# Splitting the first loads of a one-core kernel over three DMA queues

## The chip, the cores and the metric

One core of one Trainium2 chip runs the kernel. Times are device microseconds (us). Five engines work beside each other, each with its own list of instructions: TensorE (PE; its weight loads are the row PEld), VectorE (DVE), ScalarE (ACT), GpSimd (POOL) and SyncE (SP). DMA transfers are issued by SP, ACT or GpSimd, each into a queue of its own, and are carried out by 16 DMA engines. Rows with a "q" behind the engine (SPq, ACTq) are issues or waits of an engine's sequencer.

## What is computed

The input x has 2048 rows of 512. A gate per row mixes two branches:

```python
x = A_x
g = _sigmoid((x * gate_w).sum(-1, keepdims=True))
a = _A_ref(x, A_Lambda_re, A_Lambda_im, A_B_re, A_B_im, A_C_re, A_C_im, A_log_dt, A_Dskip)
b = _B_ref(x, B_wqkv, B_w_phi, B_wo)
return g * a + (1 - g) * b
```

Branch A is a diagonal complex state space model with 512 states: `Bu = x B_bar^T`, a recurrence `h = Lam_bar * h + Bu[t]` over the 2048 rows, and `y = 2 Re(h C^T) + x * Dskip`. Branch B is linear attention with 32 heads of 16: q, k and v come from `x @ wqkv`; q and k go through `w_phi` and a pair of softmaxes (of p and of -p); `kv` and `z` are sums over all rows; the output is `num / den` times `wo`. All inputs are bf16.

## The kernel before

**Tiling.** The rows are dealt by their place modulo 8, and 16 tiles of 128 rows (x0 to x15) are loaded by DMA transposes into `xT` (partition = input column). The helper `x_load(ti)` at L228 issues one such transpose on SP's queue. B's weight halves (real and imaginary, 512 KB each) go to `Bn` and from there, by eight more DMA transposes, to `BT`.

**An order written by hand.** The steps are generators (`st_...`), and the string `ORDER` (L24) lists them in the order in which their parts are emitted. The order of instructions on TensorE, VectorE, ScalarE and SP is the order of emission; GpSimd's instructions are placed by the scheduler. A token such as `W1@0` runs the next part of step W1 with PSUM bank 0; `:D` puts an eviction on VectorE instead of ScalarE; `F:4` emits four filler products (128x128 on a tile of ones, L812) that nobody reads. Every DMA issue is in order on its engine too.

**The opening.** Before the string is read, L164 issues K's weight in two halves (256 KB each, into a tile named C2r) on ACT's queue, L166 issues `w_phi` (16 KB, into Wc) on SP's, L167 preloads a ScalarE table, L236 to L240 issue x0 to x3, V's weight `Wv` (512 KB) and x4 to x7 on SP's queue, and L251 issues five small loads (vec_n, vec_m) on GpSimd's. In the string:

- `NR`, `NI` (st_N, L283) issue the two halves of B on SP's queue; `l8` to `l15` issue the other x tiles; `R0` to `R7` (st_BT, L287) the transposes of B.
- `B` (L342) builds BD, a block-diagonal matrix of w_phi, on VectorE. `W0` to `W3` (L271) transpose K's weight on TensorE; `f0` to `f3` (fold, L428) multiply it by BD, which gives Wk2.
- `V` (L308) transposes vec_n on TensorE and copies it to `vec`: the decay's parameters. `P`, `P2` to `P4`, `U` and `i0` to `i3` work on it on VectorE and ScalarE.
- `k0` to `k15` and `v0` to `v15` (tile_mm, L473) are four products of 128x512 each on one x tile; `x0`, `n0`, `e0`, `s0` and so on are the softmax features of groups of tiles (two, two, four, four, four), on VectorE and ScalarE; `a0` (L571) is the first product on features (kvacc). `g00` and so on (L597) are branch A's products on BT.
- `M` (L379) is a chain of small operations on GpSimd: powers of the decay. Three of them (r2_, r4_, r8_, L397 to L399) depend on step P alone. `D` (L417) is the reader of M's result on VectorE (dg).

Of the kernel before, what the change touches and what calls it, by code (L numbers as in the profile page):

```python
# [10 lines left out]
ALU = mybir.AluOpType  # L11
# [9 lines left out]
P = 128  # L21
MAGIC = 12582912.0
Z_MAX = 70.0
ORDER = """  # L24
NR F:28 NI B W1@0 W0@1 W0 W2@2 W1:D W3@3 W3 f1@4 W2:D f0@5 f2@6 f0 f1:D l10 V@0 F:4 V P f3@1 f3 f2:D F:4 P P k1@2 k1
l13 P2 k0@3 P2 U P2 P2 P2 P2 P4 k2@4 P3 P3 k3@5 P4 P4 k0 v0@0 i0 i2 U i0 i0 i1 i2 k4@7 i0:D i0 k2 i2 i2:D i2 U k3 k5@6
i1 v3@1 n0 x0 l9 i1 V2@2 i3 l12 x0 k4 v2@3 i3 i3 l14 i1 k5 n0 x0 n0 x0 i3 k7@4 n0 x0 U n0 i1 l11 k6@5 n1 x1 x1 n1 x1
n1 l8 R0 R1 x1 i3 k7 M v7@7 x1 n1 n1 k6:D L V2 v1@6 x2 n2 e0 v6@4 v5@5 v4@2 e0 x2 s0 v0 l15 n2 s0 n2 v2 s0 v1 R2 s0 v6
v3 n2 k10@0 k10 s0 k9@3 k9 C4 k13@6 gw D R3 s0 k12@4 e1 v7 s0 e1 s1 C6 k11@1 k11 x2 s1 k14@0 k8@3 k12 k14 k8 v4 k13
# [39 lines left out]
def kernel(  # L69
# [18 lines left out]
    nc = tc.nc  # L88
    _, S, D = A_x.shape
# [6 lines left out]
    NR = 8  # L96
# [29 lines left out]
    def order_after(ins, earlier, why):  # L126
        tc.add_manual_dep(ins.ins, earlier.ins.name, NOSYNC, reason=why)

    def pin_act_set():
        pre = nc.scalar.preload_act_table_set(ACT_SET)  # L130
        for s_ in act_st["sins"]:
            order_after(pre, s_, "table set after trig")
        act_st["pre"] = pre
        act_st["sins"] = []
        act_st["exps"] = []

    def aexp(**kw):
        ins = nc.scalar.activation(**kw)  # L138
        order_after(ins, act_st["pre"], "Exp/Ln after table-set preload")
        act_st["exps"].append(ins)  # L140
        return ins
# [19 lines left out]
    Wv = const.tile([P, KT, D], BF16, name="Wv")  # L161
    wk_nat = const.tile([P, KT, D], BF16, name="C2r")
    C2r = wk_nat
    for k0 in (0, 2):  # L164
        nc.scalar.dma_start(out=wk_nat[:, k0:k0 + 2, :], in_=B_wqkv[k0 * P:(k0 + 2) * P, D:2 * D].rearrange("(k p) n -> p k n", p=P))
    nc.sync.dma_start(out=Wc[:], in_=B_w_phi.rearrange("(k hl) e f -> (hl e) k f", hl=8))  # L166
    pin_act_set()  # L167

    xT = const.tile([P, KT, S], BF16, name="xT")
    Wo = const.tile([P, KT, D], BF16, name="Wo")  # L170
# [8 lines left out]
    G = const.tile([P, NTI], F32, name="G")  # L179
# [28 lines left out]
    Bn = pBC.tile([P, NT2, D], BF16, name="Bn")  # L208
# [19 lines left out]
    def x_load(ti):  # L228
        nc.sync.dma_start_transpose(out=xT[:, :, ti * P:(ti + 1) * P], in_=x_res[ti // 2, ti % 2])  # L229
# [3 lines left out]
    make_identity(nc, identf[:])  # L233
    mask16 = stg.tile([P, 8], BF16, name="mask16", bufs=1)
    nc.vector.tensor_reduce(out=mask16[:], in_=identf[:].rearrange("p (g e) -> p g e", e=16), axis=AX.X, op=ALU.max)
    for ti in range(4):  # L236
        x_load(ti)
    nc.sync.dma_start(out=Wv[:], in_=B_wqkv[:, 2 * D:3 * D].rearrange("(k p) n -> p k n", p=P))
    for ti in range(4, 8):
        x_load(ti)  # L240
    fk_g = tc.tile_pool(name="featK", bufs=3, reuse_waits="tile")
    fk = fk_g.__enter__()
# [21 lines left out]
    dt_, r_, om_, t0, t1, t2, den_, r2_, r4_, om8, r8_ = (par[:, 10 + k, :] for k in range(11))  # L264
    GT = nc.gpsimd.tensor_tensor
    m16 = maskN[:].rearrange("p a b -> p (a b)")
    order = [2 * g + q for g in ORD for q in range(2)]
    live = {}
# [12 lines left out]
        yield  # L281

    def st_N(ri):  # L283
        nc.sync.dma_start(out=Bn[ri * 64:(ri + 1) * 64, :, :], in_=(A_B_re, A_B_im)[ri].rearrange("(t p) d -> p t d", p=64))  # L284
        yield

    def st_BT(t):  # L287
# [16 lines left out]
    def st_O():  # L304
        nc.sync.dma_start(out=Wo[:], in_=B_wo.rearrange("(k p) n -> p k n", p=P))
        yield

    def st_V():  # L308
        pvt = bank([P, 12], BF16, "pvt")
        nc.tensor.transpose(pvt[:], vec_n[:], ident[0:12, 0:12])  # L310
        yield
        nc.vector.tensor_copy(out=vec[:, 0:3, :].rearrange("p n j -> p (n j)"), in_=pvt[:])
        yield
# [61 lines left out]
    def st_gw():  # L375
        nc.vector.tensor_copy(out=gw_b[:], in_=vec[:, 4, :])
        yield

    def st_M():  # L379
        GS = nc.gpsimd.tensor_scalar  # L380
        GC = nc.gpsimd.tensor_copy

        def cross(a, b):
            GT(out=outer, in0=a.unsqueeze(2).to_broadcast([P, 2, 2, PT]), in1=b.unsqueeze(1).to_broadcast([P, 2, 2, PT]), op=ALU.mult)

        def cmul(k, a, b):
            cross(a, b)
            GT(out=dl[:, k, :], in0=outer[:, 0, 0], in1=outer[:, 1, 1], op=ALU.subtract)
            GT(out=dl[:, k + 1, :], in0=outer[:, 0, 1], in1=outer[:, 1, 0], op=ALU.add)

        lb, m2, m4 = dl[:, 0:2, :], dl[:, 2:4, :], dl[:, 4:6, :]
        GT(out=dl[:, 0, :], in0=cs_, in1=r_, op=ALU.mult)
        GT(out=dl[:, 1, :], in0=sn_, in1=r_, op=ALU.mult)
        cmul(2, lb, lb)
        cmul(4, m2, m2)
        cmul(6, m2, m4)
        GT(out=r2_, in0=r_, in1=r_, op=ALU.mult)  # L397
        GT(out=r4_, in0=r2_, in1=r2_, op=ALU.mult)
        GT(out=r8_, in0=r4_, in1=r4_, op=ALU.mult)  # L399
        cross(lb, lam)  # L400
        GT(out=tb[:, 0, :], in0=outer[:, 0, 0], in1=outer[:, 1, 1], op=ALU.subtract)
        GT(out=tb[:, 1, :], in0=outer[:, 0, 1], in1=outer[:, 1, 0], op=ALU.add)
        GT(out=tb, in0=tb, in1=lam, op=ALU.subtract)
        GT(out=dl[:, 9, :], in0=tb[:, 0, :], in1=den_, op=ALU.mult)
        GT(out=dl[:, 8, :], in0=tb[:, 1, :], in1=den_, op=ALU.mult)
        lo = dl[:, 0:10, :].rearrange("p (k t) j -> p k t j", t=2)
        up = dl[:, 10:20, :].rearrange("p (k t) j -> p k t j", t=2)
        GS(out=up[:, 0:4, 0], in0=lo[:, 0:4, 1], scalar1=-1.0, scalar2=None, op0=ALU.mult)
        GC(out=up[:, 0:4, 1], in_=lo[:, 0:4, 0])
        GS(out=up[:, 4, 0], in0=lo[:, 4, 0], scalar1=-1.0, scalar2=None, op0=ALU.mult)  # L410
        GC(out=up[:, 4, 1], in_=lo[:, 4, 1])
        for h in range(2):
            for ri in range(2):
                GC(out=dgB[ri * 64:(ri + 1) * 64, :, :, h], in_=dl[h * 64:(h + 1) * 64, 10 * ri:10 * ri + 10, :])
        yield

    def st_D():  # L417
        v5_ = dgv.rearrange("p (k t a) f -> p k t a f", k=4, a=2)
        b5_ = dgB[:, 0:8].rearrange("p (k a) j h -> p k a (j h)", a=2)
        for a in range(2):  # L420
            nc.vector.tensor_copy(out=v5_[:, :, :, a, :], in_=b5_[:, :, a, :].unsqueeze(3).to_broadcast([P, 4, NT2, 4]))
        VT(out=idn2[:], in0=ident[:, 0:64], in1=ident[:, 64:P], op=ALU.add)
        VT(out=dg[:].rearrange("p k t (a c f) -> p (k t a) c f", f=4, a=2),
           in0=idn2[:].rearrange("p (c f) -> p c f", f=4).unsqueeze(1).to_broadcast([P, 8 * NT2, 16, 4]),
           in1=dgv.unsqueeze(2).to_broadcast([P, 8 * NT2, 16, 4]), op=ALU.mult)
        yield
# [250 lines left out]
    def st_G():  # L677
        VS(out=nge[:], in0=live["acc"][1][:, 4 * KVW:4 * KVW + NTI], scalar1=-Z_MAX, scalar2=-1.0, op0=ALU.max, op1=ALU.mult)
        yield
        aexp(out=G[:], in_=nge[:], func=ACT.Exp)  # L680
        yield
        VS(out=G[:], in0=G[:], scalar1=1.0, scalar2=None, op0=ALU.add)
        yield
        nc.vector.reciprocal(out=G[:], in_=G[:])
        yield

    def st_Y():
        for b in range(2):
# [72 lines left out]
    def st_t(n):  # L761
# [8 lines left out]
        else:  # L770
# [5 lines left out]
    small1, big1 = (lambda: sk), (lambda: fk)  # L776
    small3, big3 = (lambda: pools["sq"][1]), (lambda: pools["eq"][1])
    st = {"V": st_V(), "V2": st_V2(), "U": st_U(), "P": st_P(), "P2": st_P2(), "P3": st_P3(), "P4": st_P4(), "B": st_B(), "gw": st_gw(),
          "M": st_M(), "D": st_D(), "L": st_L(), "G": st_G(), "Y": st_Y(), "END": st_END(), "NR": st_N(0), "NI": st_N(1), "O": st_O()}
    for n in range(8, NTI):  # L780
        st[f"l{n}"] = st_l(n)
    for j in range(4):
# [65 lines left out]
```

## Time and profile before

| | |
|---|---|
| Time, median of 3 runs | 155.59 us (154.87 to 156.52) |
| Span of the profiled execution | 153.2 us |
| Busy: PE, PEld | 146.2 us (95%), 95.0 us (62%) |
| Busy: DVE, ACT, POOL | 132.4 us (86%), 129.2 us (84%), 15.8 us (10%) |
| Mean granted TensorE clock | 0.995 |
| Moved by DMA | 17.55 MB, mean 115 GB/s |

The profile is of one execution. A timeline row gives the start, the duration (of a merged group, from its first start to its last end), engine, line, operation, tiles (out<-in, buffer numbers left out), shapes, count, and in brackets the engine's idle time before it and what ended it. A busy TensorE isn't TensorE at its peak: products overlap, and a 128x512 product shown with 379 ns can follow the one before it after 216 ns.

### The profile page before, as it was taken

The page shows a single profiled execution, that of the slowest core. Times are in us where ns is not written, and L with a number is a line of the kernel's source. Part 1 is how long each engine was busy: PE and PEld are TensorE (multiplying, and loading weights), DVE is VectorE, ACT ScalarE, POOL GpSimd, SP SyncE. Part 2 cuts the span into 40 slices and gives each one's busy share as a digit, 9 for nine tenths or more (in the row PEclk, how much of TensorE's full clock was granted, in tenths as well). Part 3 has the DMA queues.
Part 4 walks back from the last instruction along what each step waited for, and adds up shares of the span by engine and source line. Part 5 has one row for each costly group of instructions (what it writes and reads, how often), then busy time and mean ns, then how long its engine had stood idle before and what let it go on. Part 6 is the DMA issues. An engine that isn't in the chain of part 4 may idle for free.

```text
span 153.2 us, 3361 instructions
## 1 busy us (share of the span) xinstructions
PE 146.2 (95%) x1236; PEld 95.0 (62%) x1254; DVE 132.4 (86%) x303; ACT 129.2 (84%) x279; POOL 15.8 (10%) x43
## 2 busy tenths in 40 slices
PE   7899999999999999999999999999999999999990
PEld 7644434788878985869867656555554455555540
DVE  3799999999999999999999999999999958717520
ACT  3489998999998999999998999699498998627562
POOL 8239980000000000000000000000000000000000
PEclk9999999999999999999999999999999999999997
DMA  4875995534445699930000007711278859969842
GB/s 116 164 218 97 223 178 112 103 75 103 103 107 78 129 230 178 166 115 4 0 0 4 0 0 169 74 37 34 42 98 147 176 122 189 162 129 206 247 143 103
DMA packets 50848, 17.55 MB, mean 115 GB/s; under 512 B 44176, under 2 KB 50832, under 8 KB 50832
## 3 DMA queue, kind: packets, MB, share of 16 engines
q1 hardware_dynamic: 48976, 15.75, 53.8%
q10 hardware_dynamic: 1696, 1.57, 3.2%
q8 instruction: 10, 0.16, 0.5%
q0 software_dynamic: 160, 0.01, 0.2%
q14 instruction: 6, 0.05, 0.1%
HBM read 2.64 MB, written 2.10 MB: 31 GB/s over the span
## 4 chain that ended last, share of the span: by engine, by line
PE 78%; SPq 10%; DMA 7%; issue 1%; ACT 1%
PE pgq L601 18%; PE py L717 16%; PE pq L475 9%; PE py L765 8%; SPq L229 8%; PE pv L475 4%; PE ph L668 4%; PE pk L475 4%; DMA xT<-in_A_x_dram 4%; PE kvacc L578 3%; DMA phT<-EEq 3%; PE pn L736 3%; PE pgq L606 2%; PE py L722 2%; PE pgq L608 2%; SPq L284 1%
## 5 line engine op out<-in xcount | busy, mean ns | idle before, releaser
L601 PE MATMUL pgq<-xT,BT 128*128 128x256 bf16 x256 | 31.5, 272 | 0.0
L475 PEld LDWEIGHTS <-xT 128*128 128x128 bf16 x192 | 18.2, 98 | 18.3 <-DMA xT<-in_A_x_dram 0.7
L601 PEld LDWEIGHTS <-BT 128*128 128x128 bf16 x256 | 24.6, 98 | 4.1
L138 ACT ACTIVATE EEk<-EEk 128x1024 bf16<-128x1024 bf16 x20 | 20.4, 1080 | 0.0
L119 ACT CAST uv<-pgq 128x512 bf16<-128x512 f32 x28 | 15.9, 605 | 0.5 <-PE pgq L601 0.4
L475 PE MATMUL pv<-Wv,xT 128*128 128x512 bf16 x59 | 15.5, 379 | 0.3
L475 PE MATMUL pq<-Wq,xT 128*128 128x512 bf16 x60 | 15.4, 379 | 0.2
L765 PE MATMUL py<-Wo,oT 128*128 128x512 bf16 x62 | 15.3, 379 | 0.1
L475 PE MATMUL pk<-Wk,xT 128*128 128x512 bf16 x62 | 14.7, 379 | 0.3 <-DMA xT<-in_A_x_dram 0.2
L138 ACT ACTIVATE EEq<-EEq 128x1024 bf16<-128x1024 bf16 x12 | 11.7, 1042 | 0.3 <-DVE EEq L527 0.3
L769 ACT ACTIVATE ot<-py,G 128x512 bf16<-128x512 f32 x12 | 7.9, 686 | 4.5 <-PE py L765 4.3
L138 ACT ACTIVATE ld<-pn 128x16 f32<-128x16 f32 x32 | 6.1, 191 | 5.7 <-PE pn L736 4.6
L590 ACT ACTIVATE phT<-X,dgB 128x512 bf16<-128x512 bf16 x16 | 10.7, 725 | 0.0
L119 ACT CAST nu<-pn 128x256 bf16<-128x256 f32 x27 | 9.9, 380 | 0.0
L119 ACT CAST vx<-pv 128x512 bf16<-128x512 f32 x16 | 9.1, 604 | 0.4 <-PE pv L475 0.4
L548 DVE TENSOR_TENSOR EEk<-EEk,rck 128x4096 bf16<-128x4096 bf16 (+1 forms) x5 | 9.3, 1858 | 0.0
L744 DVE TENSOR_TENSOR on<-nu,rd 128x512 bf16<-128x512 bf16 x16 | 6.7, 421 | 2.8 <-ACT rd L138 1.6
L765 PEld LDWEIGHTS <-oT 128*128 128x128 bf16 x64 | 5.7, 97 | 5.3 <-DMA oT<-on 0.5
L119 ACT CAST Xq<-pq 128x512 bf16<-128x512 f32 x16 | 8.9, 608 | 0.0
L119 ACT CAST Xq<-pk 128x512 bf16<-128x512 f32 x15 | 8.6, 598 | 0.4 <-PE pk L475 0.4
L736 PEld LDWEIGHTS <-phT 128*128 128x128 bf16 x128 | 6.2, 97 | 3.8 <-DMA phT<-EEq 1.4
L511 DVE TENSOR_TENSOR smk<-smk 128x512 bf16<-128x512 bf16 (+4 forms) x18 | 8.1, 448 | 0.1
(178 smaller groups left out, 321.2 us busy)
## 6 DMA issues: line engine op xcount, KB each, us to landing
X<-HM SPq DMA_DIRECT2D x8, 256.0 KB, 4.5
out_dram<-ot ACTq DMA_DIRECT2D x8, 128.0 KB, 2.5
out_dram<-ot SPq DMA_DIRECT2D x8, 128.0 KB, 2.2
C2r<-in_B_wqkv_dram ACTq DMA_DIRECT2D x2, 256.0 KB, 3.8
Wv<-in_B_wqkv_dram SPq DMA_DIRECT2D x1, 512.0 KB, 4.0
Bn<-in_A_B_re_dram SPq DMA_DIRECT2D x1, 512.0 KB, 5.7
Bn<-in_A_B_im_dram SPq DMA_DIRECT2D x1, 512.0 KB, 6.8
Wo<-in_B_wo_dram SPq DMA_DIRECT2D x1, 512.0 KB, 4.3
```

The costliest lines, as they stand in the source:

```text
L119: nc.scalar.copy(out=out_ap, in_=in_ap)
L138: ins = nc.scalar.activation(**kw)
L229: nc.sync.dma_start_transpose(out=xT[:, :, ti * P:(ti + 1) * P], in_=x_res[ti // 2, ti % 2])
L475: MM(out=pt[:], lhsT=xT[:, kt, ti * P:(ti + 1) * P], rhs=W[:, kt, :], start=(kt == 0), stop=(kt == KT - 1))
L511: VT(out=dst, in0=cur[:, :, :, 0:n, :], in1=cur[:, :, :, n:2 * n, :], op=op)
L548: VT(out=E5, in0=E5, in1=rc.to_broadcast([P, L, 2 * NB, Dh, 4]), op=ALU.mult)
L590: nc.scalar.mul(out=t_, in_=x_, mul=c_)
L601: MM(out=pg[:, h, :], lhsT=BT[:, kt, 2 * j + h, :], rhs=xT[:, kt, r * NC:(r + 1) * NC], start=(h == 0 and kt == 0), stop=(r % 2 == 0 and k ...
L717: MM(out=py[:], lhsT=hs(r, t, slice(a * P, (a + 1) * P)), rhs=C2B[t], start=(t == 0), stop=False)
L736: MM(out=pn[:, 4 * m:4 * m + 4, :].rearrange("p h e -> p (h e)"), lhsT=ph[:, 4 * hf + m, :], rhs=KVm[:, 4 * hf + m, :], start=(m == 0), st ...
L765: MM(out=py[:], lhsT=oT[:, g, :], rhs=Wo[:, g, :], start=False, stop=(g == HG - 1))
L769: nc.scalar.mul(out=ot[:], in_=py[:], mul=G[:, ti:ti + 1])
```

## The change

K's weight is issued in two halves on two queues at once: the first on ACT's, the second as the first issue of SP's, ahead of w_phi. V's weight moves from the middle of SP's x tiles to ACT's queue, right behind the table preload. The halves of B move from SP's queue to GpSimd's, behind the three powers of the decay, which become a step of their own, MP. SP's queue then carries x0 to x7 without a break. In the string, NR and NI stand behind MP, k0 comes before k1, and of the eight filler products around V and P two are left.

```diff
 ORDER = """
-NR F:28 NI B W1@0 W0@1 W0 W2@2 W1:D W3@3 W3 f1@4 W2:D f0@5 f2@6 f0 f1:D l10 V@0 F:4 V P f3@1 f3 f2:D F:4 P P k1@2 k1
-l13 P2 k0@3 P2 U P2 P2 P2 P2 P4 k2@4 P3 P3 k3@5 P4 P4 k0 v0@0 i0 i2 U i0 i0 i1 i2 k4@7 i0:D i0 k2 i2 i2:D i2 U k3 k5@6
+F:28 B W1@0 W0@1 W0 W2@2 W1:D W3@3 W3 f1@4 W2:D f0@5 f2@6 f0 f1:D l10 V@0 V P f3@1 f3 f2:D F:2 P P k0@2 k0 l13 MP NR
+NI P2 k1@3 P2 U P2 P2 P2 P2 P4 k2@4 P3 P3 k3@5 P4 P4 k1 v0@0 i0 i2 U i0 i0 i1 i2 k4@7 i0:D i0 k2 i2 i2:D i2 U k3 k5@6
...
-    for k0 in (0, 2):
-        nc.scalar.dma_start(out=wk_nat[:, k0:k0 + 2, :], in_=B_wqkv[k0 * P:(k0 + 2) * P, D:2 * D].rearrange("(k p) n -> p k n", p=P))
+    for q_, k0 in ((nc.scalar, 0), (nc.sync, 2)):
+        q_.dma_start(out=wk_nat[:, k0:k0 + 2, :], in_=B_wqkv[k0 * P:(k0 + 2) * P, D:2 * D].rearrange("(k p) n -> p k n", p=P))
     nc.sync.dma_start(out=Wc[:], in_=B_w_phi.rearrange("(k hl) e f -> (hl e) k f", hl=8))
     pin_act_set()
+    nc.scalar.dma_start(out=Wv[:], in_=B_wqkv[:, 2 * D:3 * D].rearrange("(k p) n -> p k n", p=P))
...
-    for ti in range(4):
-        x_load(ti)
-    nc.sync.dma_start(out=Wv[:], in_=B_wqkv[:, 2 * D:3 * D].rearrange("(k p) n -> p k n", p=P))
-    for ti in range(4, 8):
+    for ti in range(8):
         x_load(ti)
...
     def st_N(ri):
-        nc.sync.dma_start(out=Bn[ri * 64:(ri + 1) * 64, :, :], in_=(A_B_re, A_B_im)[ri].rearrange("(t p) d -> p t d", p=64))
+        ld_ = nc.gpsimd.dma_start(out=Bn[ri * 64:(ri + 1) * 64, :, :], in_=(A_B_re, A_B_im)[ri].rearrange("(t p) d -> p t d", p=64))
+        order_after(ld_, live["r8"], "B behind the decay's powers in GpSimd's order")
         yield
...
+    def st_MP():
+        GT(out=r2_, in0=r_, in1=r_, op=ALU.mult)
+        GT(out=r4_, in0=r2_, in1=r2_, op=ALU.mult)
+        live["r8"] = GT(out=r8_, in0=r4_, in1=r4_, op=ALU.mult)
+        yield
+
     def st_M():
...
-        GT(out=r2_, in0=r_, in1=r_, op=ALU.mult)
-        GT(out=r4_, in0=r2_, in1=r2_, op=ALU.mult)
-        GT(out=r8_, in0=r4_, in1=r4_, op=ALU.mult)
```

More of the change, by code (lines that the diff above doesn't have):

```diff
@@ L778 @@
     st = {"V": st_V(), "V2": st_V2(), "U": st_U(), "P": st_P(), "P2": st_P2(), "P3": st_P3(), "P4": st_P4(), "B": st_B(), "gw": st_gw(),
-          "M": st_M(), "D": st_D(), "L": st_L(), "G": st_G(), "Y": st_Y(), "END": st_END(), "NR": st_N(0), "NI": st_N(1), "O": st_O()}
+          "M": st_M(), "MP": st_MP(), "D": st_D(), "L": st_L(), "G": st_G(), "Y": st_Y(), "END": st_END(), "NR": st_N(0), "NI": st_N(1), "O": st_O()}
     for n in range(8, NTI):
```

## The prediction

> **What bounds the kernel now.** I read the page first, then the busy time by stretches, then the timelines of VectorE, TensorE, the issuing queues and GpSimd over the first 28 us, last the DMA packets of single stretches.
>
> ```profile
> span 153.2 us, 3361 instructions
> ```
>
> The profiled execution's own time is taken as this span with what lies around it. The median of the runs, 155.59, is 2.4 us above the span, and I keep that 2.4 for the changed kernel.
>
> Busy time by stretches (columns: stretch and length; busy us of PE, PEld, DVE, ACT, POOL, with counts; clock, DMA share, GB/s):
>
> ```profile
> core 0: us, PE busy (x) PEld busy (x) DVE busy (x) ACT busy (x) POOL busy (x), PEclk, DMA share, GB/s
> 10.00:16.00 6.00, 6.00 (x29) 2.65 (x28) 5.90 (x24) 5.99 (x17) 4.77 (x8) 1.00 0.72 154
> 16.00:22.00 6.00, 5.95 (x29) 2.73 (x28) 5.87 (x16) 5.97 (x11) 5.47 (x19) 1.00 1.26 181
> 22.00:28.00 6.00, 5.84 (x28) 2.38 (x26) 5.93 (x13) 5.42 (x12) 0.77 (x1) 1.00 0.64 132
> 28.00:34.50 6.50, 6.50 (x76) 5.53 (x75) 6.50 (x13) 6.50 (x14) 0.00 (x0) 1.00 0.43 85
> ```
>
> The reader is to see VectorE's column: between 10 and 34.5 us it is idle for 0.10 + 0.13 + 0.07 + 0.00 = 0.30 us only. TensorE is as full, at full clock. Two engines run in step. This is where they meet (PE and its weight loads):
>
> ```profile
> 22.89 5.35 PE L475 MATMUL pk<-Wk,xT 128*128 128x512 bf16 x24 [0.16 <-DMA xT<-in_A_x_dram]
> ```
> ```profile
> 28.20 0.30 PEld L578 LDWEIGHTS <-EEk 128*128 128x128 bf16 x8 [0.46 <-DVE EEk L548]
> ```
>
> At 22.89 TensorE waits for an x tile (x9), which looks like a bound by SP's queue. But at 28.20 it waits again, 0.46 us, for VectorE's features. Whatever is won on x tiles before that is waited away there, because VectorE, with 0.30 us of air, is not earlier. So the question is what sets the start of VectorE's full stretch.
>
> ```profile
> 3.97 0.69 DVE L343 TENSOR_TENSOR BD<-Wc,mask 128x512 bf16<-128x512 bf16 x1 [1.16 <-DMA Wc<-in_B_w_phi_dram]
> 5.13 0.91 DVE L121 COPY Xq<-ptw 128x512 bf16<-128x512 bf16 x2 [0.47 <-PE ptw L274]
> 6.06 0.69 DVE L121 CAST Wk<-pf 128x512 bf16<-128x512 f32 x1
> 7.10 0.17 DVE L312 CAST vec<-pvt 128x12 f32<-128x12 bf16 x1 [0.34 <-PE pvt L310]
> 7.18 0.68 DVE L121 CAST Wk<-pf 128x512 bf16<-128x512 f32 x1
> ```
>
> VectorE's order is fixed by hand: first BD (step B, which needs w_phi in Wc), then two copies of K's transposed weight, one fold's cast, then vec at 7.10, from which the whole decay chain and all later work follow. Two waits lie in this opening, 0.47 and 0.34 us. The second is for step V's product:
>
> ```profile
> 4.54 1.25 PE L274 MATMUL ptw<-ident,C2r 128*128 128x128 bf16 x16 [0.26 <-DMA C2r<-in_B_wqkv_dram]
> ...
> 6.90 0.16 PE L310 MATMUL pvt<-ident,vec_n 12*128 12x12 bf16 x1 [0.29 <-DMA vec_n<-in_A_log_dt_dram]
> 6.99 0.40 PE L812 MATMUL spin<-fillw 128*128 128x128 bf16 x4
> ...
> 7.67 3.62 PE L475 MATMUL pk<-Wk,xT 128*128 128x512 bf16 x15
> ```
>
> So today the opening is set by GpSimd's small load vec_n, at about 6.8 us, with K's weight and w_phi some tenths behind it.
>
> **The change part by part.** The queues of before (SP, then ACT, then the page's line on K's load: KB each, us from issue to landing):
>
> ```profile
> 0.79 0.45 SPq L166 DMA_DIRECT2D Wc<-in_B_w_phi_dram  x1
> 1.31 5.21 SPq L229 DMA_TRANSPOSE xT<-in_A_x_dram  x4
> 6.57 0.58 SPq L238 DMA_DIRECT2D Wv<-in_B_wqkv_dram  x1
> 7.19 5.12 SPq L229 DMA_TRANSPOSE xT<-in_A_x_dram  x4
> 12.36 1.28 SPq L284 DMA_DIRECT2D Bn<-in_A_B_re_dram  x1
> 13.69 0.62 SPq L284 DMA_DIRECT2D Bn<-in_A_B_im_dram  x1
> 14.36 9.97 SPq L229 DMA_TRANSPOSE xT<-in_A_x_dram  x7
> ```
> ```profile
> 0.79 1.07 ACTq L165 DMA_DIRECT2D C2r<-in_B_wqkv_dram  x2
> 1.89 1.28 ACT L130 ACT_TABLE_LOAD   x1 [1.89 <-issue]
> ```
> ```profile
> C2r<-in_B_wqkv_dram ACTq DMA_DIRECT2D x2, 256.0 KB, 3.8
> ```
>
> *SP's issues.* K's second half takes 1.07 / 2 = 0.53 us ahead of everything. So w_phi is issued at 1.32 instead of 0.79 and the first four instead of 0.79 and the first four; the next four, without V's weight (0.62 from 6.57 to 7.19), 0.1 earlier; the rest, without B's halves (2.0 from 12.36 to 14.36), 2.1 earlier. What that can pay is the x9 wait and no more than the 0.30 us of air in VectorE. I enter 0.1.
>
> *K's weight and w_phi: the term that decides.* How do two queues share the engines? From 2.8 to 3.5 us, K (ACT's queue, q10) and w_phi (SP's, q1) run side by side:
>
> ```profile
> q10 hardware_dynamic: 227, 0.22, 97.3%
> q1 hardware_dynamic: 192, 0.01, 15.7%
> ```
>
> That is 227 packets against 192, nearly one for one, though one kind has 1 KB and the other 32 bytes. By the shares, with 16 engines over 0.7 us, a packet costs 0.973 x 11.2 / 227 = 48 ns and 0.157 x 11.2 / 192 = 9.2 ns. So w_phi (16 KB, 512 packets) alone takes 512 x 9.2 / 16 = 0.29 us of all engines, and beside a stream of 1 KB packets 512 x (48 + 9.2) / 16 = 1.83 us.
>
> After, w_phi stands behind 256 KB of K on its own queue, and when its turn comes, ACT's queue has V's weight (512 KB, 512 packets of 1 KB) ready. ACT's DMA isn't held up by the table load issued before it, to judge by the late part of the kernel, where the issue at 129.70 starts while the cast before it still runs:
>
> ```profile
> 129.52 0.39 ACT L119 CAST nu<-pn 128x256 bf16<-128x256 f32 x1
> 129.70 0.36 ACTq L773 DMA_DIRECT2D out_dram<-ot  x1
> ```
>
> Today K's second half is issued at 1.33 and lands 3.8 later, at 5.1. Its packets are through a little earlier, an estimate of 4.5 from that landing; without w_phi among them, 4.2. Then w_phi: 4.2 + 1.83 + 0.3 for its landing = 6.3, instead of 3.97 where BD starts today. Bounds: if V's weight did not alternate with it, 4.2 + 0.29 + 0.4 = 4.9; if K's landing less 0.29 is the start, 4.8 + 1.83 = 6.7. I take 6.3, nearest to the row of 227 and 192.
>
> [...]
>
> *From w_phi to vec.* Today 7.10 - 3.97 = 3.13 us, of which 0.47 + 0.34 are waits: 2.3 us of work in order (BD 0.69, two copies 0.91, cast 0.69). The fold's products need a copy and BD, and V's product stands behind three folds on TensorE, so nothing of it overtakes. After: 6.3 + 2.3 = 8.6, against 7.10: +1.5 us (bounds 4.9 + 2.3 = 7.2: +0.1; 6.7 + 2.3 = 9.0: +1.9). The landing of vec_n, near 6.8, is then covered, and so is the first half of K, which now shares the engines with the second and lands some 0.3 later than 4.5.
>
> *Does +1.5 reach the end?* VectorE has 0.30 us of air up to 34.5, TensorE none after 28.2, so yes; I take the 0.1 above off.
>
> *Six fillers.* Four take 0.40 at most, so six at most 0.6; they stand in waits for fold casts, which after the change are longer. Nothing. K tile 0 ahead of tile 1 follows the landing order: nothing.
>
> *V's weight.* First read by pv after three k tiles, near 11 us; it is issued 5 us sooner. Nothing, except through w_phi.
>
> *B's halves on GpSimd* (GpSimd's timeline; VectorE's reader; the time to landing of a small GpSimd load; the DMA packets from 14.5 to 19.3, when B's load runs; and TensorE's products on x7 and x6):
>
> ```profile
> 8.97 0.23 POOL L399 TENSOR_TENSOR ssm_par<-ssm_par 128x4 f32<-128x4 f32 x1
> ...
> 11.82 1.18 POOL L392 TENSOR_TENSOR dl<-ssm_par 128x4 f32<-128x4 f32 x1
> ...
> 19.74 1.98 POOL L414 COPY dgB<-dl 64x40 f32<-64x40 f32 x4
> ```
> ```profile
> 24.72 2.29 DVE L423 TENSOR_TENSOR dg<-idn,phT 128x4096 bf16<-128x4096 bf16 x1
> ```
> ```profile
> vec_n<-in_A_log_dt_dram POOLq DMA_DIRECT2D x1, 1.0 KB, 3.5
> ```
> ```profile
> q1 hardware_dynamic: 1008, 1.02, 103.2%
> ```
> ```profile
> 15.65 1.89 PE L475 MATMUL pk<-Wk,xT 128*128 128x512 bf16 x8
> ```
>
> The three powers already run at 8.4 to 9.2 today, before the rest of step M, so the new step MP moves nothing. The two issues come behind them, at 9.2 + 1.5 = 10.7. B's transfer fills the engines for 1.03 x 4.8 = 5.0 us, so it lands by 10.7 + 3.5 + 5.0 = 19.2 or a few us later when x tiles run beside it; SP reaches its first reader, BT, near 22. Queued behind the issues on GpSimd is step M, whose last copy ends at 21.7; the reader on VectorE (two casts before 24.72) comes 2.5 us later. The issue of so many rows from GpSimd is in no row here; from zero to those 2.5 us it costs nothing.
>
> Sum: 153.2 + 1.5 - 0.1 = 154.6 of span, +2.4 = **157.0 us**.
>
> **The rivals.**
>
> *w_phi isn't late (chance 0.20).* If ACT's queue delivers V's packets only after the table load (1.28 us), or w_phi isn't alternated, it lands near 4.9 and vec is still held by vec_n. VectorE's line stays, and only its air and the x9 wait are to be had: 0 to 0.5 us. For it: no row shows a DMA issued right behind a table load. Against it: the issue at 129.70. Time 155.1 to 155.7, not slower; it decides as long as w_phi lands before 7.1 - 2.3 = 4.8 to 4.9.
>
> [...]
>
> *B on GpSimd collides with x tiles (0.15).* Today B stands behind x7 on the same queue; after, it runs beside x6 and x7. TensorE wants x7 at 15.65 (17.1 with the shift), and B ends at 19.2 by the sum above: a wait of up to 2.1 us, in TensorE's order with nothing to fill it, less the 0.5 that it waits at 28.2 anyway. Or GpSimd itself is slow: a product of 4 columns took 1.18 us at 11.82 and 0.23 at 8.97, so something stretches its work when VectorE is full; with more than 2.5 us for the two issues VectorE's dg waits. Either costs up to 1.6 more: 157.2 to 158.6. Against it: x7 is issued before B's packets can be there. [...]
>
> **How the numbers follow.** Forecast 0.55, and 0.20, 0.10, 0.15 for the rivals. One per cent is 1.56 us, about what the runs of 154.87 to 156.52 can tell from nothing: the borders are 154.0 and 157.15. The forecast spans 155.7 to 157.5 and lies over the upper border with 0.4 of its chance (0.22); the collision with 0.85 of its own (0.13); together 0.35, with a little for a TensorE that cools in the longer opening 0.37. Faster by 1% needs 1.56 us where 0.5 are to be had: 0.06 for what I don't see. The rest, 0.57, is within. Range 155.0 to 158.2: below it is the better part of the gain (0.08), above it the worse half of the collision.
>
> **What would show it.** BD on VectorE starts near 6.3 with a long wait for w_phi, and vec near 8.6; TensorE idles between the transposes and the first fold; no wait for x9 any more, but a longer one for VectorE at the first kvacc product, now near 29.6. The forecast is wrong if BD starts before 5, if vec stays near 7.1, or if the shift at the first kvacc product isn't found again at the end. A wait of TensorE for x7 or x6 would speak for the collision.

## The result, and the profile after

| | before | after |
|---|---|---|
| Time, median (lowest to highest), 4 runs each | 155.58 us (154.87 to 156.52) | 161.56 us (160.93 to 161.97) |
| Ratio to before, 95% interval | | 1.0377 [1.0334, 1.0421] |
| Span of the profiled execution | 153.2 us | 160.0 us |
| Mean granted clock | 0.995 | 0.977 |

The change makes the kernel slower by 3.8%, some 5.9 us. The forecast was 157.0 in a range of 155.0 to 158.2. Ratios leave disturbed executions out; where a run below has none, its executions lay too far apart for one.

The page of the changed kernel, the span, the packets by queue, and the group of K's products (busy us and mean ns, idle time before, what ended it):

```profile
span 160.0 us, 3352 instructions
...
PEclk9999957999999999999999999999999999999999
...
q0 software_dynamic: 448, 1.05, 3.2%
...
L477 PE MATMUL pk<-Wk,xT 128*128 128x512 bf16 x62 | 16.4, 411 | 3.6 <-DMA xT<-in_A_x_dram 3.5
```

A queue q0 (GpSimd's) has B's 1.05 MB. The clock has two lower digits in slices six and seven, 20 to 28 us. K's products have an idle time of 3.6 us, nearly all of it one wait for an x tile.

**The opening.** VectorE's timeline of the changed kernel, then the one wait of TensorE in it that matters:

```profile
5.18 0.69 DVE L342 TENSOR_TENSOR BD<-Wc,mask 128x512 bf16<-128x512 bf16 x1 [2.49 <-DMA Wc<-in_B_w_phi_dram]
...
8.32 0.17 DVE L311 CAST vec<-pvt 128x12 f32<-128x12 bf16 x1 [0.93 <-PE pvt L309]
```
```profile
8.12 0.16 PE L309 MATMUL pvt<-ident,vec_n 12*128 12x12 bf16 x1 [0.94 <-DMA vec_n<-in_A_log_dt_dram]
```

BD starts at 5.18 (3.97 before; 6.3 in the prediction). What holds vec at 8.32 is GpSimd's small load vec_n, which now lands at 7.98 instead of 6.76. Why is seen in the DMA packets between 2 and 5 us, first before, then after (packets, MB, share of 16 engines; a load's us from issue to landing):

```profile
q10 hardware_dynamic: 544, 0.52, 54.8%
q1 hardware_dynamic: 1168, 0.19, 40.9%
q0 software_dynamic: 66, 0.00, 1.6%
...
vec_n<-in_A_Lambda_im_dram POOLq DMA_DIRECT2D x1, 1.0 KB, 3.6
```
```profile
q10 hardware_dynamic: 525, 0.52, 50.2%
q1 hardware_dynamic: 785, 0.26, 36.6%
...
vec_n<-in_A_Lambda_im_dram POOLq DMA_DIRECT2D x1, 1.0 KB, 5.0
```

Before, 66 packets of GpSimd's queue get through by 5 us; after, none, though the loads are issued at the same place in GpSimd's order.

**B against x7.** GpSimd's timeline (B's two issues), SP's issues (x4 to x7), the packets between 13 and 16.5 us, and TensorE's products on x6 and x7, all of the changed kernel:

```profile
10.20 0.76 POOL L282 DMA_DIRECT2D Bn<-in_A_B_re_dram  x1
10.96 0.70 POOL L282 DMA_DIRECT2D Bn<-in_A_B_im_dram  x1
```
```profile
7.08 5.20 SPq L230 DMA_TRANSPOSE xT<-in_A_x_dram  x4
```
```profile
q0 software_dynamic: 204, 0.77, 102.0%
q1 hardware_dynamic: 73, 0.01, 3.6%
```
```profile
15.81 1.04 PE L477 MATMUL pv<-Wv,xT 128*128 128x512 bf16 x4
20.31 3.60 PE L477 MATMUL pk<-Wk,xT 128*128 128x512 bf16 x8 [3.46 <-DMA xT<-in_A_x_dram]
```

x7 is the last of SP's four transposes and issued at 11.02, within 0.1 us of B's second half. From 13 to 16.5 us the packets of GpSimd's queue fill the engines: 204 of them, 0.77 MB, 3.8 KB each on average. SP's queue gets 73 packets in, 0.01 MB (44 of x's 256 bytes, the others of 4). x7 lands at 20.26 instead of 14.71, and TensorE stands still for 3.46 us, up to 20.31.

B's second half lands at 18.36, x7 1.9 us later. Something else is in flight near x7's end, as the packets from 16.5 to 18.2 us show:

```profile
q1 hardware_dynamic: 578, 0.14, 79.9%
q0 software_dynamic: 47, 0.13, 41.5%
q8 instruction: 1, 0.02, 4.7%
```

The last row is a load of instructions, 16 KB in one packet, which starts at 18.00 and takes 1.3 us (4.7% of 16 engines for 1.7 us). From 18.75 to 19.95 us next to nothing moves, 25 packets of SP's queue, and x7 lands right behind them. In two runs below x7 landed 0.6 us after the last of B on GpSimd's queue (16.66 after 16.04, and 19.45 after 18.88). By an estimate from these, B alone would have let x7 land near 19.0 here, and some 1.3 us of the wait are the instructions'. No run varied their load by itself.

**What follows from the wait.** Busy time by stretches of the changed kernel (PE, PEld, DVE, ACT, POOL, then the clock, DMA share, GB/s), and VectorE's wait:

```profile
18.00:20.00 2.00, 0.00 (x0) 0.00 (x0) 1.93 (x8) 0.32 (x1) 1.86 (x8) 0.85 1.43 64
20.00:22.00 2.00, 1.69 (x5) 0.59 (x6) 0.84 (x3) 0.00 (x0) 0.11 (x1) 0.50 1.47 199
22.00:24.00 2.00, 2.00 (x6) 0.75 (x5) 0.06 (x1) 1.75 (x2) 0.00 (x0) 0.50 0.58 121
24.00:26.00 2.00, 2.00 (x6) 0.76 (x5) 1.97 (x4) 1.99 (x3) 1.08 (x1) 0.50 0.46 98
26.00:28.00 2.00, 1.95 (x10) 0.82 (x9) 2.00 (x5) 1.85 (x5) 0.00 (x0) 0.95 0.55 109
```
```profile
23.94 0.69 DVE L121 CAST Xq<-pk 128x512 bf16<-128x512 f32 x1 [3.06 <-PE pk L477]
```
```profile
35.30 0.42 PE L580 MATMUL kvacc<-vx,EEk 128*128 128x68 bf16 x8
```

TensorE's clock is granted at 0.50 from 20 to 26 us: six products fall in each 2 us from 22 to 26, against 10 and more in 2 us at full clock. By the 0.85 of the first row it fell some 0.6 us before 20, that is 2.5 us into the wait. VectorE, the saturated engine of before, starves for 3.06 us. The first kvacc product comes at 35.30 instead of 28.20, and the 7 us of shift stay nearly whole to the end (160.0 - 153.2 = 6.8).

### The profile page after: what moved, and what is told of

Read it like the earlier page. It is cut to its first block, busy times and chain, and to the rows that moved or that the text cites. A ratio compares the mean times of both kernels' runs of the same rounds, so it can differ in the third digit from the quotient of the medians.

```text
span 160.0 us, 3352 instructions
## 1 busy us (share of the span) xinstructions
PE 148.9 (93%) x1230; PEld 95.8 (60%) x1248; DVE 133.0 (83%) x303; ACT 129.8 (81%) x279; POOL 14.4 (9%) x45
## 3 DMA queue, kind: packets, MB, share of 16 engines
q0 software_dynamic: 448, 1.05, 3.2%
## 4 chain that ended last, share of the span: by engine, by line
PE 82%; SPq 6%; DMA 6%; ACT 2%; issue 1%; DVE 1%
PE pgq L603 18%; PE py L719 17%; PE pq L477 9%; PE pv L477 8%; PE py L767 7%; PE pk L477 7%; DMA xT<-in_A_x_dram 6%; SPq L230 6%; PE ph L670 4%; PE kvacc L580 3%; PE pn L738 3%; PE py L724 2%; PE pgq L608 2%; PE pgq L610 2%; PE ph L669 1%
## 5 line engine op out<-in xcount | busy, mean ns | idle before, releaser
L477 PEld LDWEIGHTS <-xT 128*128 128x128 bf16 x192 | 18.9, 101 | 23.9 <-issue 4.1
L477 PE MATMUL pk<-Wk,xT 128*128 128x512 bf16 x62 | 16.4, 411 | 3.6 <-DMA xT<-in_A_x_dram 3.5
L477 PE MATMUL pv<-Wv,xT 128*128 128x512 bf16 x59 | 16.8, 404 | 0.3
```

Of the source, the lines that this page charges most:

```text
L477: MM(out=pt[:], lhsT=xT[:, kt, ti * P:(ti + 1) * P], rhs=W[:, kt, :], start=(kt == 0), stop=(kt == KT - 1))
```

## The experiments

The theory after the result: B's packets on GpSimd's queue starve the x tiles on SP's queue, TensorE idles for x7 and then runs at half clock; this is some 4.4 us of the 5.9. The rest, 1.5, is V's weight, which delays vec_n. Rivals: w_phi behind K's half is the 1.5, as predicted; the clock is not part of the price; what costs is GpSimd's queue as such, not B's traffic at this place. "K tile 7" is the product on x7.

| kernel | median us | ratio, interval | vec | x7 lands | K tile 7 starts | first kvacc |
|---|---|---|---|---|---|---|
| before | 155.6 | | 7.10 | 14.71 | 15.65 | 28.20 |
| after | 161.56 | 1.0377 [1.0334, 1.0421] | 8.32 | 20.26 | 20.31 | 35.30 |
| e1_b_on_sp | 157.2 | 1.0096 [1.0061, 1.0132] | 8.47 | 13.96 | 16.84 | 29.63 |
| e7_k_split_only | 156.47 | 1.0049 [1.0014, 1.0084] | 7.39 | 14.49 | 15.78 | 28.51 |
| e12_half_b | 157.6 | 1.0104 [1.0067, 1.0141] | 8.71 | 16.66 | 17.29 | 29.86 |
| e4_b_later | 157.82 | 1.0117 [1.0036, 1.0198] | 8.79 | 16.07 | 17.16 | 30.98 |
| e9_fill_70 | 161.91 | 1.0364 [1.0307, 1.0422] | 8.34 | 21.14 | 21.41 | 33.29 |
| e13_fill_long | 160.25 | 1.0301 [1.0254, 1.0349] | 8.55 | 20.76 | 21.03 | 32.90 |

(The ratios are to the kernel before, run beside each on the same chip, with medians of 155.49 to 155.77. The last four columns are of the one profiled execution, which isn't always a median one: it took 155.64 us for e7_k_split_only and 161.03 for e13_fill_long.)

**B's halves back on SP's queue (e1_b_on_sp).**

```diff
-        ld_ = nc.gpsimd.dma_start(out=Bn[...], in_=...)
-        order_after(ld_, live["r8"], ...)
+        nc.sync.dma_start(out=Bn[...], in_=...)
-F:28 B W1@0 ... l13 MP NR NI P2
+NR F:28 NI B W1@0 ... l13 MP P2
```

> B's halves go back to SP's queue behind x7; all else as changed. Theory: the 6 us come from a chain of three: V's weight on ACT's queue makes vec_n land 1.2 us later (vec at 8.3 instead of 7.1), B on GpSimd starves x7 (TensorE waits 3.5 us at k7), and that wait halves TensorE's clock for some 6 us. Here only the first is left: vec near 8.3, no wait at k7, clock 1.00 throughout, 156.6 to 157.3 us. Rival (the wait at k7 and the clock come from the missing fillers, the order k0 before k1 or the crowded opening): TensorE still waits or cools, 159 us or more.

157.2 us. TensorE of this run, at K tile 7 and at the first kvacc product:

```profile
16.84 1.89 PE L476 MATMUL pk<-Wk,xT 128*128 128x512 bf16 x8
...
29.63 0.43 PE L579 MATMUL kvacc<-vx,EEk 128*128 128x68 bf16 x8 [0.34 <-DVE EEk L549]
```

No wait, eight products in 1.89 us (3.60 after), and the first kvacc product where the prediction had put it, 29.6. So B on GpSimd costs 161.56 - 157.2 = 4.4 us, and the rest of the change 1.5.

**V's weight back between x3 and x4, B left on GpSimd.**

```diff
-    nc.scalar.dma_start(out=Wv[:], in_=...)
-    for ti in range(8):
+    for ti in range(4):
+        x_load(ti)
+    nc.sync.dma_start(out=Wv[:], in_=...)
+    for ti in range(4, 8):
         x_load(ti)
```

> V's weight goes back between x3 and x4 on SP's queue; B stays on GpSimd. Theory: vec_n lands near 6.8 again and vec is back at 7.1 to 7.3, but x7 is issued 0.6 us later and B 1.2 earlier, so the wait at k7 and the half clock stay: 160 to 162 us. Rival (V's weight is the main cause): 158 us or less.

162.55 (159.82 to 164.25; the profile is of the fastest). vec comes at 7.69 instead of 8.32, but x5 is late too (TensorE waits 1.11 us at 14.53) and x7 costs a wait of 1.99 us, with 3.4 us of half clock behind it. What V's weight gives back at the start is lost again to B, by these rows; as its executions lie far apart, the run says nothing of V's weight by itself.

**Only the split of K, k0 ahead of k1, MP and fewer fillers (e7_k_split_only).** The edits of the two runs above together.

> Of the change only K's weight on two queues, K tile 0 ahead of tile 1, the powers in a step of their own and six fillers fewer; V's weight and B's halves are on SP's queue as before. Theory (the rest of the loss, 1.5 us, is V's weight ahead of the small GpSimd loads): vec_n lands near 6.8 to 7.3, vec near 7.6, held by w_phi's landing near 5.5; 155.7 to 156.5. Rival (it is w_phi behind K's half that makes the 1.5): vec near 8.4, 157.0 to 157.5.

156.47 us, VectorE of this run:

```profile
5.27 0.69 DVE L343 TENSOR_TENSOR BD<-Wc,mask 128x512 bf16<-128x512 bf16 x1 [2.46 <-DMA Wc<-in_B_w_phi_dram]
...
7.39 0.16 DVE L312 CAST vec<-pvt 128x12 f32<-128x12 bf16 x1
```

w_phi is as late as in the changed kernel, and vec is at 7.39, not 8.3: this speaks against w_phi. vec_n lands at 6.94; with V's weight on ACT's queue, in the run with B's halves back on SP's, it landed at 8.13. These two runs differ in V's weight alone. It costs 1.1 us of vec (8.47 - 7.39), and by the medians 0.7 us of the time (157.2 - 156.47), though the intervals of the two just overlap; the split and what goes with it some 0.8 (0.0049 of 155.5).

**w_phi ahead of K's half, in the run just told.**

```diff
+    nc.sync.dma_start(out=Wc[:], ...)
     for q_, k0 in ((nc.scalar, 0), (nc.sync, 2)):
         q_.dma_start(out=wk_nat[:, k0:k0 + 2, :], ...)
-    nc.sync.dma_start(out=Wc[:], ...)
```

> The run with K's split alone (V's weight and B's halves on SP's queue), and w_phi ahead of K's second half on SP's queue. Theory (what the split alone costs, 1.0 us by its medians, is w_phi's landing at 5.24 instead of 3.94, which moves vec by 0.3, and little else): w_phi lands near 4, BD starts near 4.0, vec at 6.9 to 7.2, 155.3 to 155.9. Rival (the cost lies in the later x tiles and K's halves, not in w_phi): vec at 7.1 all the same, 156.2 to 156.8.

156.23 us (155.03 to 157.04), 1.0032 [0.9999, 1.0065]. VectorE of this run:

```profile
3.90 0.69 DVE L343 TENSOR_TENSOR BD<-Wc,mask 128x512 bf16<-128x512 bf16 x1 [1.09 <-DMA Wc<-in_B_w_phi_dram]
...
7.30 0.17 DVE L312 CAST vec<-pvt 128x12 f32<-128x12 bf16 x1
```

BD starts 1.37 us earlier and vec 0.09: vec_n lands at 6.95 in both. So w_phi's lateness is worth a tenth of a microsecond of vec here. Where the 0.3 to 0.5% that is left comes from stays open; vec is 0.2 later than before and the intervals of the two runs overlap.

**V's weight on ACT's queue, but behind the first eviction there (B on SP).**

```diff
-F:28 B W1@0 W0@1 W0 W2@2
+NR F:28 NI B W1@0 W0@1 W0 WV W2@2
```

> The changed kernel with B's halves back on SP's queue, and V's weight on ACT's queue behind W0's eviction, some 4 us later than in the change. Theory (V's weight holds up the small GpSimd loads and so vec): vec_n lands near 6.8 to 7.2, vec near 7.5, x9 comes no later than in the run with B on SP; 155.5 to 156.2. Rival (V's weight did nothing, the 1.5 us come from w_phi behind K's half): vec 8.3 to 8.5, 157.2.

159.37 us, a miss. ACT's timeline of this run:

```profile
9.18 0.39 ACTq L377 DMA_DIRECT2D Wv<-in_B_wqkv_dram  x1
9.61 0.58 ACT L119 COPY Xq<-ptw 128x512 bf16<-128x512 bf16 x1 [3.30 <-DMA xT<-in_A_x_dram]
```

ACT held the issue until an x tile had landed (x2, at 9.16; the last section says what the two share), and the copy of K's weight behind it, which the folds need, was held with it. vec_n did come earlier (7.47, vec 7.81 against 8.47), as the theory has it, but the time is ruled by ACT's stop.

**B on ACT's queue.**

```diff
-        ld_ = nc.gpsimd.dma_start(out=Bn[...], in_=...)
+        nc.scalar.dma_start(out=Bn[...], in_=...)
```

> B's halves on ACT's queue at about the same time as on GpSimd's (behind k0's eviction), in packets of 1 KB instead of 4 KB. Theory (the queues take turns packet by packet, so the size of the other queue's packet sets the x tiles' pace): x7 gets one packet per 1 KB instead of one per 4 KB and lands near 17, wait at k7 0.5 to 1.5 us, no cooling: 157 to 158.5 us. Rival one (any second queue starves the transposes): as changed, 161. Rival two (only GpSimd's queue does so): no wait at k7, 156.8.

163.42 us (161.82 to 164.75; the profile is of the fastest). The same thing again, on ACT:

```profile
13.96 0.69 ACTq L282 DMA_DIRECT2D Bn<-in_A_B_re_dram  x1
...
16.64 1.28 ACT L144 ACT_TABLE_LOAD   x1 [6.04 <-DMA xT<-in_A_x_dram]
```

B's first issue starts when x7 has landed (13.94), the second, at 15.99, when x8 has (15.97), and ACT does nothing else for 6 us. x7 itself was on time because B wasn't there yet, so the run doesn't say what B on another hardware queue would do to x tiles.

**B on GpSimd later (e4_b_later).** B's issues stand behind the product cmul(4) of step M, whose first part is emitted earlier for it. They start at 17.52 and 18.48, some 7 us later and not the 4 that were meant.

```diff
-        order_after(ld_, live["r8"], ...)
+        order_after(ld_, live["cmul", 4], ...)
```

> The changed kernel with B's two halves still on GpSimd, but issued behind the product cmul(4) of step M, some 4 us later (near 14 to 15 us instead of 10.2 and 11.0). Theory (the 4.4 us come from x7, which stands in SP's queue beside B's packets for one stretch, and not from GpSimd's queue as such): x7 lands near 14, TensorE doesn't wait at k7, its clock stays at 1.0, first kvacc product 29.5 to 31; 156.8 to 158.5. Rival (B on GpSimd is dear wherever it is issued, since the x tiles behind x7 are held up just as x7 was): the wait moves to k9 to k12, first kvacc product over 33, 160 to 162.

157.82 us. x7 lands at 16.07, before TensorE wants it (17.16). That is 2.1 us later than with B on SP's queue (13.96), although nothing of B is issued yet; a load of instructions starts at 14.06 here, which fits what was said of the one at 18.00. The wait moves to a later x tile and is smaller, at full clock:

```profile
28.38 2.76 PE L478 MATMUL pk<-Wk,xT 128*128 128x512 bf16 x12 [1.44 <-DMA xT<-in_A_x_dram]
```

The same load on the same queue, issued at 17.5 and 18.5, costs some 0.6 us (157.82 - 157.2; the intervals overlap) in place of 4.4. GpSimd's queue as such is not the price.

**Half of B on GpSimd (e12_half_b).** The first half as in the change, the second on SP's queue behind x7.

> The changed kernel with only the first half of B (512 KB) on GpSimd, the second on SP's queue behind x7. Theory (B's packets of 4096 bytes leave the x tiles hardly any turns for as long as there are B's packets, so x7's landing goes by how much of B is in flight): x7 lands between 13.96, where it landed with nothing of B on GpSimd, and 20.26, where it landed with all of it, near 16 to 17; TensorE waits at k7 for 0.3 to 1.5 us at most, its clock stays at 1.0; 157.2 to 158.6. [...]

157.6 us (157.47 to 157.83). x7 lands at 16.66, between 13.96 and 20.26, and TensorE, which wants it at 17.29, doesn't wait:

```profile
17.29 1.89 PE L480 MATMUL pk<-Wk,xT 128*128 128x512 bf16 x8
```

The landing goes with the amount of B in flight, as far as three points tell; the time doesn't, because TensorE has some 2.9 us in hand (16.84 - 13.96 in the run with B on SP). The first half costs nothing that the intervals tell (1.0104 against 1.0096); with the second half behind it on GpSimd's queue nearly all of the 4.4 us come at once (161.56 - 157.6 = 4.0).

**B in rows of 512 bytes.** Each half in two loads of 256 columns.

```diff
-        ld_ = nc.gpsimd.dma_start(out=Bn[...], in_=...)
+        for c_ in (0, D // 2):
+            ld_ = nc.gpsimd.dma_start(out=Bn[..., c_:c_ + D // 2], in_=...[:, c_:c_ + D // 2]...)
```

> The changed kernel with each of B's halves on GpSimd cut into two loads of 256 columns (512 bytes a row instead of rows that the queue sent in packets of 4096 bytes); four issues instead of two, some 1.5 us more of GpSimd. Theory (x7's packets of 256 bytes get a turn for each of B's packets, so the size of B's packets sets how long x7 waits): packets of 512 bytes, x7 lands near 15.5 to 17, the wait at k7 0.5 to 1.5 us, the clock falls little or not, 157.5 to 159.5. Rival (GpSimd's queue outweighs SP's whatever its packets): x7 lands near 20 or later, 161 to 163. If the packets keep more than 512 bytes, the run doesn't tell the two apart.

159.9 us (157.56 to 162.05). The packets between 13 and 16.5 us of this run:

```profile
q0 software_dynamic: 159, 0.53, 77.3%
q1 hardware_dynamic: 550, 0.13, 25.6%
```

0.53 MB in 159 packets is 3.3 KB each (130 packets of 4096 bytes, the others of 4): the queue put the shorter rows into packets of 4096 bytes as before, so the run can't tell the size of the packets from the kind of queue. That x7 landed at 18.32, earlier than with two loads, is not explained by it.

**Fillers in the wait (e3_fill_gap, e9_fill_70, e13_fill_long).** TensorE works through the wait for x7 on products that nobody reads, in the bank of K tile 7: 60 of 128 columns, then 70, then 18 of 512.

```diff
         pk = bank([P, D], F32, "pk")
+        for _ in range(70 if ti == 7 else 0):
+            MM(out=pk[:, 0:P], lhsT=fillw[:], rhs=fillw[:], start=True, stop=True)
```

> As changed, with 60 filler products (128x128, into k7's own bank before its first product) ahead of k7, some 3.4 us of TensorE that lie in its wait. Theory: the clock stays at 1.00, the 14 products that took 427 instead of 216 ns are full speed again, 3.0 us less of them; the wait at k7 stays as it is: 158.3 to 159.3 us. Rival (VectorE's own wait of 3 us governs, and the slow clock lies under it): 160.8 us or more.

> The changed kernel with 70 filler products in the bank of K tile 7, ahead of its own products: TensorE works through the wait for x7 instead of standing still. Theory (of the 4.4 us that B on GpSimd costs, some 3 are TensorE's half clock after the idle stretch, and the wait itself is less than it looks): the granted clock stays at 1.0 from 18 to 28 us, the first kvacc product comes 2 to 3 us earlier after x7's landing than the 15.0 us of the changed kernel, 158.5 to 160.5. Rival (the clock doesn't matter, the wait for x7 alone is the price): 161 to 162 whatever the clock shows.

161.9 and 161.91 us. The clock is 1.00 in every 2 us from 18 to 28 us in both profiles, and with 70 fillers the first kvacc product comes 2.0 us earlier than in the changed kernel (33.29 against 35.30), yet the time is the same. Where do 2 us go? The two kernels keep that distance up to SP's issue near 127 us (126.83 against 128.79); then come SP's issues, first with 70 fillers, then after:

```profile
126.83 3.96 SPq L762 DMA_TRANSPOSE oT<-on  x2
```
```profile
128.79 2.50 SPq L760 DMA_TRANSPOSE oT<-on  x2
```

The pair of transposes takes 3.96 us instead of 2.50. In the stretch of the longer pair (126.8 to 130.6) lies one packet that the stretch of the shorter (128.8 to 131.5) hasn't:

```profile
q8 instruction: 1, 0.02, 2.5%
```

It is again a load of instructions, 16 KB, 1.5 us long. In the changed kernel such packets come every 9 to 22 us, and TensorE starts 231 to 296 instructions from one to the next, weight loads counted. That their places go by this count is an estimate from it; 70 fillers are 140 instructions with their weight loads. A second one at 147.1 falls on another two transposes, and TensorE waits again:

```profile
149.48 0.43 PE L740 MATMUL pn<-KVm,phT 128*128 128x68 bf16 x8 [0.81 <-DMA phT<-EEq]
```

If this is so, the same fill in fewer instructions should keep the gain:

```diff
+        for _ in range(18 if ti == 7 else 0):
+            MM(out=pk, lhsT=fillw[:], rhs=xT[:, 0, 0:D], start=True, stop=True)
```

> The changed kernel with 18 filler products of 512 columns in the bank of K tile 7, in place of the 70 of 128 columns tried before: about the same time of TensorE (18 x 0.216 = 3.9 us), but 36 instructions more in its stream instead of 140. Theory (the half clock does cost 2 to 3 us, and with 70 fillers that gain was lost at the end, where the 16 KB instruction packets, moved by 140 instructions, fell at 127.5 and 147.1 us onto transposes of oT and phT that TensorE waits for): the clock stays at 1.0, first kvacc product 33 to 33.6, no such waits behind 125 us, 159.0 to 160.2. Rival (the clock is not part of the price; anything gained ahead of the tail is lost in it): 161 to 162, with the first kvacc product as early.

160.25 us, all six executions between 159.75 and 161.03. TensorE of this run:

```profile
16.92 4.05 PE L482 MATMUL pk<-xT,fillw 128*128 128x512 bf16 x18
21.03 1.67 PE L477 MATMUL pk<-Wk,xT 128*128 128x512 bf16 x7
...
32.90 0.42 PE L582 MATMUL kvacc<-vx,EEk 128*128 128x68 bf16 x8
```

From the start of K tile 7 to the first kvacc product it takes 11.87 us at full clock, 14.99 in the changed kernel: the half clock costs 3.1 us there. 2.4 us of the gain last to 138 us, 1.3 in the median; the rest goes near 139 in one wait for a transpose, in a stretch with two instruction packets, as the changed kernel has there too, but one of them 1.9 us long instead of 0.4. The time is at the upper end of what was expected. The clock is part of the price: the first kvacc product shows it, in two runs, and the time by 1.3 us (161.56 - 160.25), though the two intervals touch. That instruction packets take back the rest is what the rows suggest; of them only the place was varied, and only with the fillers.

**Eight fillers around V and P, as before.**

```diff
-V@0 V P f3@1 f3 f2:D F:2 P P
+V@0 F:4 V P f3@1 f3 f2:D F:4 P P
```

> The changed kernel with eight filler products in place of its two, at the places where the kernel before has them (four ahead of V, four ahead of the first P). Theory (the fillers stand in waits for fold casts and cost and bring nothing): as the changed kernel, 160.9 to 162.0. Rival (without them TensorE idles long enough for its clock to fall early): 0.5 to 1 us less, 160.3 to 160.8.

163.94 us (160.18 to 165.0): its executions lie too far apart to tell anything of fillers. x7's landing varies by itself (21.57 in the profile).

**vec_n first, in the kernel before.**

```diff
+    for n, src in enumerate((A_Lambda_im, A_Lambda_re, A_log_dt)):
+        nc.gpsimd.dma_start(out=vec_n[4 * n:4 * n + 4, :], in_=src.rearrange("(j p) -> j p", p=P))
     make_identity(nc, ident[:])
...
-    for t_, srcs in ((vec_n, (A_Lambda_im, A_Lambda_re, A_log_dt)), (vec_m, (A_Dskip, gate_w))):
+    for t_, srcs in ((vec_m, (A_Dskip, gate_w)),):
```

> The kernel before with the three small loads of vec_n ahead of the identity matrices in GpSimd's order, nothing else changed. Theory (vec is held by vec_n, which lands last at 6.76, while BD and what follows it leave vec free at some 6.3): vec_n lands 0.3 to 1 us earlier, vec near 6.4 to 6.9 instead of 7.10, and 0.2 to 0.6 us off the time, 154.9 to 155.3 against 155.5. Rival (the identity matrices now come later by three issues and hold up the transposes and BD by as much): vec no earlier, 155.5 to 156.5.

155.81 us, 0.9997 [0.9962, 1.0031]. VectorE of this run:

```profile
4.09 0.29 DVE L238 TENSOR_REDUCE mask<-identf 128x8 bf16<-128x128 f32 x1 [1.92 <-POOL identf masks.py:199]
...
5.01 0.69 DVE L346 TENSOR_TENSOR BD<-Wc,mask 128x512 bf16<-128x512 bf16 x1
...
7.34 0.16 DVE L315 CAST vec<-pvt 128x12 f32<-128x12 bf16 x1
```

vec_n lands 0.2 earlier (6.58), but the identity matrices come later, VectorE waits 1.92 us for them, and BD starts at 5.01. vec is 0.2 later. No version was found that beats the kernel before.

## Why the prediction was wrong

**The step that failed: B's halves on GpSimd, which the sum enters with nothing.** They cost 4.4 us, three quarters of the loss. The words "from zero to those 2.5 us it costs nothing" look at GpSimd's own time alone. The issues were seen rightly (0.76 + 0.70 us at 10.20, where 1.5 at 9.2 was assumed), GpSimd's chain M has room, and B's end came near the sum (18.4 against 19.2). What was missing was what B's transfer does to those beside it. The collision was a rival at 0.15, and it was set aside with "x7 is issued before B's packets can be there". That was checked for the issue alone. x7 is issued at 11.02, but its packets pass from 12.5 us on where B isn't beside them (the run with B on SP's queue), and in the changed kernel B's are there by then.

Part of the answer was at hand. The prediction had divided the packets by their bytes for K and w_phi, and not for B and x. An x tile is 128 KB in packets of 256 bytes, 512 of them; B's 1 MB came in 256 packets of 4096. So even at one packet for one, near the 227 and 192 of the prediction, an estimate is that only 256 packets of x pass in B's whole 5 us, half a tile. The trace shows less than that at first: from 12.5 to 15.2 us 34 packets of SP's queue, next to no data, beside 162 of GpSimd's; then, from 15.2 to 17, 74 beside 89, not far from one for one. What keeps x7's first packets back until 15.2 stays open. The size of GpSimd's packets is in no row of before; the changed kernel's trace gives it (0.77 MB in 204 is 3.8 KB).

**The rival's price was short as well.** It gave a wait of up to 2.1 us and at most 1.6 more. The wait was 3.46. By the estimate above B alone makes about 2.1 of it (19.0 - 16.85, where TensorE's wait begins), just what the rival had, and the load of instructions, which the prediction names nowhere, the rest. Behind the wait TensorE ran at half clock, 3.1 us by the fillers of 512 columns. "A TensorE that cools" was named with a little chance and no price, and for the longer opening, not for the collision. That is why the time fell outside the range.

**The +1.5 us before vec: the right size from the wrong cause.** Measured are 1.22 on vec, 1.43 on the first kvacc product with B out of the way (29.63 - 28.20), and 1.5 on the time (0.0096 x 155.5): without B on GpSimd the kernel took 157.2, and the prediction said 157.0. But w_phi landed at 5.16, not 6.3. Its packets went through from 3.8 us on, and faster than one for one; the packets of the changed kernel from 3.8 to 4.5 us:

```profile
q10 hardware_dynamic: 194, 0.18, 75.0%
q1 hardware_dynamic: 481, 0.03, 44.2%
```

The 5.16 lies between the lower bound, 4.9, and the 6.3, whose 1.83 us for one packet beside one no run shows; why w_phi's packets went faster stays open. And "the landing of vec_n, near 6.8, is then covered" was the error that made up for it: V's weight on ACT's queue, which was charged through w_phi alone, moved vec_n to 7.98. The two runs that differ in w_phi's place alone have vec at 7.30 and 7.39, the two that differ in V's weight alone at 7.39 and 8.47: that settles it. So the 157.0, right for the kernel without B on GpSimd, was luck.

**Right:** VectorE is saturated from 10 us on and a shift of vec stays to the end (in the run with B on SP TensorE waits 0.34 us for it at kvacc again, and the span is 2.0 us longer than before). SP's freed issues brought next to nothing: x8 was issued 2.0 us earlier (12.33) and landed 0.3 earlier (20.75 against 21.02). The sign named for a collision, a wait of TensorE for x7, is the one that came. **Not settled:** the six fillers, and k0 ahead of k1, which was not run by itself; and how much of x7's lateness the instructions make.

Two slips change nothing: 4.8 + 1.83 is 6.6, not 6.7, and the sentence on the first four x tiles compares w_phi's times with themselves (x0 was issued at 1.82 instead of 1.31).

## What to carry to other kernels

Before a transfer is moved to another queue, list what is in flight on all queues while it runs, and compare packets, not bytes or issues alone: here a load in large packets (4096 bytes) beside a stream of small ones (256) took nearly all of the engines (102.0% against 3.6% from 13 to 16.5 us), and the first tile that was wanted in that time paid. Keep a late-wanted load behind the early-wanted ones on one queue, or issue it when they have landed; the order within a queue is the only priority that these runs used. A wait of TensorE is to be priced with the slower clock that can follow it (0.50 for 6.8 us here), and a gain that is made by adding instructions is to be followed to the end of the kernel.

## What the runs showed of the hardware

- B came over GpSimd's queue in packets of 4096 bytes with rows of 1 KB (256 packets in the changed kernel) and with rows of 512 bytes (130 of the 159 packets from 13 to 16.5 us). From 13 to 16.5 us of the changed kernel 204 packets of this queue passed (0.77 MB) and 73 of SP's (0.01 MB), from 15.2 to 17 us 89 and 74.
- Three loads of 1 KB on GpSimd's queue landed 1.2 us later (7.98 against 6.76, 8.13 against 6.94) when V's weight, 512 KB, was on ACT's queue too; in the changed kernel no packet of theirs passed before 5 us.
- TensorE's clock fell to 0.50 some 2.5 us into the idle time of 3.46 us, and for 6.8 us. Idle times of 1.99 us (V's weight back on SP's queue) and of 2.48 us (V's weight behind the first eviction) were followed by 3.4 us of half clock, one of 2.33 us (60 fillers) by none, so the length alone doesn't tell. The wait of 2.48 us, then the stretch with the clock, 0.55, behind it:

```profile
10.25 0.61 PE L435 MATMUL pf<-BD,Xq 128*128 128x128 bf16 x4 [2.48 <-ACT Xq L119]
```
```profile
10.00:12.00 2.00, 1.75 (x9) 1.08 (x10) 1.03 (x7) 1.48 (x5) 0.25 (x2) 0.55 0.82 213
```

- An issue on ACT's queue that was added in the opening waited for x tiles of SP's queue to land (x2 in one run, x7 and x8 in the other) and held ACT for 3.3 and 6.0 us, though nothing in the data asks for that. In the trace each of the three issues counts its landing on the same semaphore as the x tile (number 107; 105 and 106), and starts 0.02 us after that tile has landed. Whether another semaphore frees it was not tried.
- A load of instructions (16 KB in one packet, 0.9 to 1.9 us) went with transposes in flight that landed later: with one at 14.06 x7 landed at 16.07, with one at 13.46, behind x7's last packets, at 13.96 (the runs with B later on GpSimd's queue and with B on SP's). This is read off the traces; it was not varied by itself.
